# Delta-rule attention into two mixtures: warm matmuls between the opening's grams, and the next half solve on VectorE

## The chip, the cores and the metric

The kernel runs on one core of one Trainium2 chip. The metric is the device time of one execution in microseconds (us), the median of the runs.

## The reference

Three parts in a row, all in float32 at the outside; the weights come as float64.

```python
def _attn_ref(q, k, v, beta):                  # 4 batches, 8 heads, 768 positions, 48 wide
    k_n = k / (np.linalg.norm(k, axis=-1, keepdims=True) + 1e-06)
    for t in range(S):
        y[:, :, t] = einsum('bhd,bhde->bhe', q[:, :, t], state)
        v_old = einsum('bhde,bhd->bhe', state, kt)
        state = state + bt * einsum('bhd,bhe->bhde', kt, vt - v_old)

def _moe_ref(x, w_gate, w_val, w_out):         # 3072 tokens, 384 -> 1536 -> 384
    g = x @ w_gate
    return ((g * sigmoid(g)) * (x @ w_val)) @ w_out

def _moe2_ref(x, w_in, w_out):                 # 3072 tokens, 384 -> 2048 -> 384
    h = x @ w_in
    return (h * tanh(softplus(h))) @ w_out
```

## The kernel before

**The attention** goes over the 768 positions in 24 chunks of 32, three chunks to a step (t = 0 to 7). The 4 batches x 32 positions of a chunk lie on the 128 partitions. Inside a chunk the recurrence is a triangular system of 32 unknowns for each batch and head. A step needs: grams of the keys (`gram_pair`, L458; word kg), the norms of the keys (in step 0 by `square_sums`, L209 and L210, later from the gram's diagonal), and the solve. In the first two steps the solve is made in two halves of 16: `solve_half` (L276, L283) makes 15 pairs of operations, one pair for each unknown, for both halves side by side; `back_half` (L287 to L289) turns the result back with three transposes; `join` (L298) puts the halves together in two parts (words ja and jb, for the next step Ja and Jb), each of 64 small products with a ScalarE copy or a VectorE add (L309) behind.

Each chunk then runs a chain: `read` (word r: keys times state, L350, and on VectorE v minus that, L362; word y: queries times state), `att_solved` (word z: solved system times v, L370, copied into z_s once by ScalarE, L380, and once by VectorE, L376, each masked to half of the batches), `att_update` (word u: ds, L412, and the state's sum on VectorE, four operations, L429), `att_out` (word o: y from the gram of queries and keys, word qg, masked on POOL by qm, L197, and z_s; L389, ScalarE copy L398), and `x_out` (word x: three transposes, L440, ScalarE's cast xh, L445, VectorE's rest xl, L447). v is scaled by the norm on POOL (word vs, L314).

**The first mixture** takes one step of 384 tokens at a time, in groups over the 12 slices of the hidden size: gate g (L635), then ScalarE's s (L678); value v (L635), then VectorE's h (L686) and its two parts hp; and down x (L707), two slices later. Every product is three passes: high part by high, low by high, high by low. g and v have one PSUM bank each (tags "g" and "v"), so a gate waits for the s before it and a value for the h before it. The weights are converted piece by piece during the opening and the first mixture: raw data by DMA (`fetch`, L546), two ScalarE operations (`conv_begin`, L561 and L563; word cb), one VectorE operation f (`conv_step`, L572; word d), then w1h on ScalarE (L591) and w1l on POOL (L592) (`conv_tail`, word t). The next attention step's work is put between the groups. **The second mixture** (from 666 us) is all matmuls.

The order of the opening is written by hand: the string START is a list of words that `say` carries out one after the other, and each engine gets its instructions in that order. A word with ">" behind it issues the first phase of a phased step and one with ">" ahead of it the next. Besides those named: turn (transpose of the gram into g_sys, L202), scale, diag, s and S (that many pairs of the solve on VectorE, of this step and of the next), P (pairs of the next step's solve on POOL), nb, ns, ne, gam (norms in pieces), clear (POOL sets t_sys to zero), h (that many warm matmuls of zeros, L826), fetch (raw pieces by ScalarE's queue), go and done (switches). EARLY1 does the same for the first mixture: "2.3:Ja2>" is carried out 0.3 of the way into group 2.

Of the kernel before, what the change touches and what calls it, by code (L numbers as in the profile page):

```python
# [7 lines left out]
F32 = mybir.dt.float32  # L8
# [4 lines left out]
AF = mybir.ActivationFunctionType  # L13
ALU = mybir.AluOpType
# [13 lines left out]
sq0 sq1 sq2 h12 kg0 kg1 norm kg2 turn0 scale diag s1 Kg0 s2 Kg1 s2 Kg2 s2 qg0 s2 qg1 s2 qg2 s5 vs0 vs1 vs2 fetch go cb2 qm0 qm1 qm2 back0 clear  # L28
ja0> ja1> >ja0 jb0> ja2> >ja1 turn1 nb d1 >jb0 z0> >ja2 jb1> ns1 y0 >z0 u0> o0> ns2 t1 >u0 >jb1 r1> jb2> y1 ne >r1 z1> gam1 >o0 >jb2 x0> d1 >z1 u1> o1> scale diag >x0 >x0 t1 P5
>u1 r2> y2 >r2 z2> >o1 x1> d1 >z2 u2> o2> >x1 >x1 P5 t1 >u2 >o2 x2> qg3 >x2 >x2 P5 d1 t1 qm3 d1 t1 done  # L30
# [11 lines left out]
XTS = ("v", "x22", "v")  # L42
AHEAD = 1
EARLY1 = "0.7:back1 1.3:Ja0> 1.3:Ja1> 1.6:>Ja0 1.6:>Ja1 2.3:Ja2> 2.3:Jb0> 2.6:>Ja2 2.6:>Jb0 3.3:Jb1> 3.3:Jb2> 3.6:>Jb1 3.6:>Jb2 4.0:qg4 4.6:qm4 6.3:qg5 7.3:qm5"
# [15 lines left out]
def tile_delta_attention_moe_moe(  # L60
# [78 lines left out]
    z_s = at.tile([128, H, 2, D], F32, name="z_s")  # L139
# [40 lines left out]
    def k_of(n):  # L180
        return lent_k if n == 2 else k_s[n % 2]
# [183 lines left out]
    def att_solved(t, c):  # L365
# [18 lines left out]
    def att_out(t, c, hold):  # L384
        y = hold["y"]
        for h in range(H):
            for b in range(B):
# [4 lines left out]
                    rhs=z_s[bs, h, b % 2, :],  # L392
# [9 lines left out]
    def att_update(t, c):  # L402
        n = num(t, c)
        if starting:
            pss = [psm.tile([128, NP, 2, D], F32, tag=x, name="ds") for x in ("g", "x20")]
        else:
            pss = [psa.tile([128, NP, 2, D], F32, tag="a", name="ds") for _ in range(2)]
        for p in range(NP):
            for par in range(2):
                for x in range(2):  # L410
# [4 lines left out]
                        rhs=z_s[rows, 2 * p + par],  # L415
# [402 lines left out]
    fetch(0, nc.sync)  # L818
    fetch(1, nc.sync)
# [257 lines left out]
```

## Time and profile before

| | us |
|---|---|
| median of three runs | 1077.2 (1076.88 to 1077.98) |
| time of the profiled execution | 1075.51 |
| its span in the trace | 1073.4 |
| TensorE busy | 1031.5 (96%) |
| VectorE busy | 512.9 (48%) |
| ScalarE busy | 398.3 (37%) |
| POOL (GpSimd) busy | 190.2 (18%) |
| granted TensorE clock, mean over the span | 0.974 |

PE is TensorE's matmuls, DVE is VectorE, ACT is ScalarE, POOL is GpSimd, SP issues most DMAs. The granted clock is 1.00 at 2.4 GHz and 0.50 at 1.2 GHz. In a timeline row "x32" joins that many like instructions that follow each other; the time is from the first's start to the last's end, and the bracket tells how long the engine had been idle and what released it. "issue" there is a wait for nothing that the profile shows. The profile counts a small float32 product twice, as two matmuls; the lists of instructions below count it once. In the windows view a row gives the stretch, its length, and for each of PE, PEld (weight loads), DVE, ACT and POOL the busy time and the number of instructions, then the granted clock, the share of the DMA engines and GB/s; with one engine asked for, that engine alone.

### The profile page before, as it was taken

The numbers are of one execution on the slowest core, as the hardware profiler recorded it, in microseconds if no ns is written. First come the engines' busy times: TensorE is split into PE (matmuls) and PEld (weight loads), VectorE is DVE, ScalarE is ACT, GpSimd is POOL, SyncE is SP. The second block draws the span as 40 slices with busy tenths as digits, with TensorE's granted clock in tenths as the row PEclk, the third lists the DMA queues.
The fourth block names the chain that finished last, engine by engine and source line by source line (L and its number), as shares of the span: only waits on it lengthen the run. The fifth ranks groups of instructions, "written<-read, shape, count | busy, mean of one in ns | idle before, by whom it ended". The sixth has DMA issues, their size and how long they took to land.

```text
span 1073.4 us, 29430 instructions
## 1 busy us (share of the span) xinstructions
PE 1031.5 (96%) x12980; PEld 988.7 (92%) x12980; DVE 512.9 (48%) x1113; ACT 398.3 (37%) x871; POOL 190.2 (18%) x222
## 2 busy tenths in 40 slices
PE   4779799999999999999999999999999999999998
PEld 4668699889989999999999999999999999999998
DVE  8555896785884885866852243212121222212111
ACT  2259744224224234243222345333333333323232
POOL 3276632211211312212211121000000000000000
PEclk6779899999999999999999999999999999999999
DMA  7246624215206125132010044001000000100000
GB/s 213 93 152 211 202 85 154 72 45 167 72 32 188 45 72 154 44 109 68 16 60 2 16 148 140 23 7 39 24 23 23 23 31 16 38 7 30 1 23 23
DMA packets 43183, 77.52 MB, mean 72 GB/s; under 512 B 4272, under 2 KB 30000, under 8 KB 43056
## 3 DMA queue, kind: packets, MB, share of 16 engines
q1 hardware_dynamic: 41904, 72.50, 21.6%
q10 hardware_dynamic: 1152, 3.15, 0.9%
q8 instruction: 102, 1.67, 0.7%
q14 instruction: 25, 0.20, 0.1%
HBM read 59.90 MB, written 15.73 MB: 70 GB/s over the span
## 4 chain that ended last, share of the span: by engine, by line
PE 81%; DVE 6%; issue 1%; ACT 1%; ACTq 0%; DVEq 0%
PE o L635 19%; PE h L635 19%; PE v L635 12%; PE x L707 12%; PE g L635 11%; PE z L370 1%; PE ks L350 1%; PE ds L412 1%; PE y L389 1%; PE y L350 1%; DVE t_tmp L324 1%; PE gram L458 1%; DVE t_sys L331 1%; DVE h L686 1%; DVE state L429 1%
## 5 line engine op out<-in xcount | busy, mean ns | idle before, releaser
L983 DVE TENSOR_TENSOR gl<-gg,gh 128x384 fp32r<-128x384 f32 x128 | 71.4, 558 | 319.2 <-ACT gh L982 319.2
L692 POOL TENSOR_TENSOR hp<-h,hp 128x384 fp32r<-128x384 f32 x96 | 99.8, 1039 | 419.4 <-ACT hp L691 419.4
L977 ACT ACTIVATE gg<-h 128x384 f32<-128x384 f32 x128 | 62.9, 492 | 264.8 <-PE h L635 264.8
L707 PE MATMUL x<-hp,w1h 128*128 128x384 f32 x576 | 132.1, 338 | 1.4 <-ACT hp L691 1.4
L635 PE MATMUL o<-w2l,gh 128*128 128x384 f32 x384 | 129.3, 337 | 0.0
L635 PE MATMUL o<-w2h,gh 128*128 128x384 f32 x384 | 129.2, 336 | 0.0
L635 PE MATMUL o<-w2h,gl 128*128 128x384 f32 x384 | 129.2, 336 | 0.0
L691 ACT CAST hp<-h 128x384 fp32r<-128x384 f32 x96 | 49.3, 513 | 168.5 <-DVE h L686 168.4
L707 PEld LDWEIGHTS x<-hp,w1h 128*128 128x128 f32 x576 | 101.1, 188 | 3.9 <-ACT hp L691 2.1
L635 PE MATMUL h<-x2h,w2h 128*128 128x384 f32 x384 | 88.0, 337 | 0.0
L635 PE MATMUL h<-x2l,w2h 128*128 128x384 f32 x384 | 87.8, 336 | 0.0
L635 PE MATMUL h<-x2h,w2l 128*128 128x384 f32 x384 | 87.7, 336 | 0.0
L686 DVE TENSOR_TENSOR h<-s,v 128x384 f32<-128x384 f32 x96 | 52.8, 549 | 72.7 <-PE v L635 72.1
L678 ACT ACTIVATE s<-g 128x384 f32<-128x384 f32 x96 | 46.9, 489 | 101.6 <-PE g L635 101.6
L324 DVE TENSOR_TENSOR t_tmp<-t_sys,g_sys 128x31 f32<-128x31 f32 (+15 forms) x186 | 80.9, 435 | 4.5
L331 DVE TENSOR_TENSOR t_sys<-t_sys,t_tmp 128x31 f32<-128x31 f32 (+15 forms) x186 | 74.8, 402 | 6.4
L635 PE MATMUL g<-xh,w1h 128*128 128x384 f32 x288 | 69.2, 349 | 7.5 <-ACT s L678 6.5
L635 PEld LDWEIGHTS o<-w2h,gh 128*128 128x128 f32 x384 | 72.1, 188 | 0.0
L635 PEld LDWEIGHTS o<-w2h,gl 128*128 128x128 f32 x384 | 72.1, 188 | 0.0
L635 PEld LDWEIGHTS o<-w2l,gh 128*128 128x128 f32 x384 | 72.1, 188 | 0.0
L635 PE MATMUL v<-xh,w1h 128*128 128x384 f32 x288 | 67.8, 343 | 2.9 <-DVE h L686 2.6
L635 PEld LDWEIGHTS h<-x2h,w2h 128*128 128x128 f32 x384 | 68.9, 188 | 0.0
(129 smaller groups left out, 1762.9 us busy)
## 6 DMA issues: line engine op xcount, KB each, us to landing
raw<-in_w_second_dram SPq DMA_DIRECT2D x32, 384.0 KB, 4.0
raw<-in_w_first_dram SPq DMA_DIRECT2D x28, 384.0 KB, 3.9
kqT<-in_kq_dram SPq DMA_DIRECT2D x18, 512.0 KB, 3.6
w2d<-f SPq DMA_DIRECT2D x32, 192.0 KB, 4.1
w2raw<-w2d SPq DMA_DIRECT2D x16, 384.0 KB, 2.9
v<-in_v_dram SPq DMA_DIRECT2D x24, 192.0 KB, 2.9
x2d<-xs SPq DMA_DIRECT2D x24, 192.0 KB, 1.9
x2raw<-x2d SPq DMA_DIRECT2D x24, 192.0 KB, 2.4
```

The source lines that it names most:

```text
L324: nc.vector.tensor_tensor(out=tmp, in0=t_sys[:, 0:m, j:j + 1].to_broadcast([128, m, n]), in1=g_sys[:, j:j + 1, j + 1:C].to_broadcast([128, ...
L331: nc.vector.tensor_tensor(out=sl, in0=sl, in1=tmp, op=ALU.subtract)
L350: nc.tensor.matmul(out=ps[bs, 2 * p:2 * p + 2], lhsT=kqt[:, p, w, bs], rhs=state[:, b, p], start=not w or p == 0, stop=not w, skip_group_c ...
L370: nc.tensor.matmul(out=z[bs, h], lhsT=t_of(t)[bs, :, c * H + h], rhs=v_s[c][bs, h, :], start=True, stop=True)
L635: nc.tensor.matmul(out=ps, lhsT=a, rhs=b, start=start and i == 0, stop=stop and i == len(seq) - 1)
L678: nc.scalar.activation(out=s, in_=ps, func=AF.Silu)
L686: nc.vector.tensor_tensor(out=h, in0=g_t.pop(j), in1=ps, op=ALU.mult)
L691: nc.scalar.copy(out=hh, in_=h)
L692: nc.gpsimd.tensor_tensor(out=hl, in0=h, in1=hh, op=ALU.subtract)
L707: nc.tensor.matmul(out=x2[kk], lhsT=w[j][:, 6 + kk, :], rhs=m, start=j == 0 and i == 0, stop=j == J1 - 1 and i == 2,)
L977: nc.scalar.activation(out=gg, in_=ps, func=AF.Mish)
L983: nc.vector.tensor_tensor(out=gl, in0=gg, in1=gh, op=ALU.subtract)
```

## The change

1. The squares of the keys (sq) are made by ScalarE instead of VectorE.
2. 48 more warm matmuls stand between the first six and the last three grams of the opening (h18, h6, h8, h8, h5, h3), and 11 later (h2, h3, h6).
3. vs and qm (POOL) stand behind back0 and clear instead of beside the solve.
4. The next step's half solve is made by VectorE (S1, S2, S2, S2, S3 in the opening, S5 in the first mixture) instead of POOL (P5 three times); its back1 and joins come later in the first mixture.
5. jb2 moves from ahead of y1 to behind o1; o2 goes ahead of u2; the third state update (">u2"), gram qg3 and its mask qm3 move into the first mixture, and six weight pieces instead of five are converted ahead of it.
6. Raw pieces 2 and 3 are fetched by SP's queue at the start, ahead of three loads of kqT, instead of by ScalarE's queue in the opening ("fetch").
7. z_s holds its two halves one behind the other instead of interleaved by head, and the third chunk's ds and the xt use other PSUM banks.

```diff
--- before.py
+++ after.py
@@ -25,9 +25,9 @@
 FIRST = 0
 FB = 3
 START = """
-sq0 sq1 sq2 h12 kg0 kg1 norm kg2 turn0 scale diag s1 Kg0 s2 Kg1 s2 Kg2 s2 qg0 s2 qg1 s2 qg2 s5 vs0 vs1 vs2 fetch go cb2 qm0 qm1 qm2 back0 clear
-ja0> ja1> >ja0 jb0> ja2> >ja1 turn1 nb d1 >jb0 z0> >ja2 jb1> ns1 y0 >z0 u0> o0> ns2 t1 >u0 >jb1 r1> jb2> y1 ne >r1 z1> gam1 >o0 >jb2 x0> d1 >z1 u1> o1> scale diag >x0 >x0 t1 P5
->u1 r2> y2 >r2 z2> >o1 x1> d1 >z2 u2> o2> >x1 >x1 P5 t1 >u2 >o2 x2> qg3 >x2 >x2 P5 d1 t1 qm3 d1 t1 done
+sq0 sq1 sq2 h12 kg0 kg1 norm kg2 h18 turn0 scale diag s1 Kg0 h6 s2 Kg1 h8 s2 Kg2 h8 s2 qg0 h5 s2 qg1 h3 s2 qg2 s5 go cb2 back0 clear vs0 qm0 vs1 qm1 vs2 qm2
+ja0> ja1> >ja0 jb0> ja2> >ja1 turn1 nb d1 >jb0 z0> >ja2 jb1> ns1 y0 >z0 t1 u0> o0> ns1 >u0 >jb1 h2 r1> y1 ns1 ne >r1 z1> >o0 h3 gam1 scale diag d1 S1 >z1 t1 u1> o1> jb2> S2 d1
+>u1 >jb2 r2> x0> y2 S2 >x0 >r2 >x0 >o1 t1 z2> x1> S2 d1 >z2 o2> u2> >x1 >x1 t1 >o2 x2> h6 d1 >x2 >x2 t1 S3 d1 t1 done
 """
 FILL = (0.1, 0.8)
 W2AT = (4.5, 2.0, 6)
@@ -39,9 +39,9 @@
 MOST = 2
 GRAMS = ("g", "x20", "x21", "x22") * 5
 JOINS = ("x21", "x22") * 3
-XTS = ("v", "x22", "v")
+XTS = ("x22",) * 3
 AHEAD = 1
-EARLY1 = "0.7:back1 1.3:Ja0> 1.3:Ja1> 1.6:>Ja0 1.6:>Ja1 2.3:Ja2> 2.3:Jb0> 2.6:>Ja2 2.6:>Jb0 3.3:Jb1> 3.3:Jb2> 3.6:>Jb1 3.6:>Jb2 4.0:qg4 4.6:qm4 6.3:qg5 7.3:qm5"
+EARLY1 = "0.3:S5 0.9:back1 1.2:qg3 1.4:qm3 1.6:>u2 2.9:Ja0> 2.9:Ja1> 3.2:>Ja0 3.2:>Ja1 3.6:Ja2> 3.6:Jb0> 3.9:>Ja2 3.9:>Jb0 4.3:Jb1> 4.3:Jb2> 4.6:>Jb1 4.6:>Jb2 5.0:qg4 5.3:qm4 7.0:qg5 7.3:qm5"
 GRAM2 = 6.0
 
 
@@ -136,7 +136,7 @@
     ss, rs, n_sys = [t_tmp[:, C * i:C * i + C] for i in range(3)]
     state = at.tile([128, B, NP, 2, D], F32, name="state")
 
-    z_s = at.tile([128, H, 2, D], F32, name="z_s")
+    z_s = at.tile([128, 2, H, D], F32, name="z_s")
     y_s = [at.tile([128, DM], F32, name=f"y{i}") for i in range(NCH)]
 
     w2d = [dram.tile([128, 6, 128], F32, name=f"w2d{j}") for j in range(J2)]
@@ -204,9 +204,9 @@
         )
 
     def square_sums(c):
-        sq = m1.tile([128, H, D], F32, tag="h", name="sq")
-        kk = k_of(c)
-        nc.vector.tensor_tensor(out=sq, in0=kk, in1=kk, op=ALU.mult)
+        sq = m1.tile([128, 2, N], F32, tag="hp", name="sq", bufs=2)
+        sq = sq[:, 0].rearrange("p (h d) -> p h d", h=H)
+        nc.scalar.activation(out=sq, in_=k_of(c), func=AF.Square)
         nc.vector.tensor_reduce(out=n_nat[:, c * H:c * H + H], in_=sq, op=ALU.add, axis=mybir.AxisListType.X)
 
     def norms(diag):
@@ -374,10 +374,10 @@
         for x in range(2):
             if starting and x:
                 nc.vector.tensor_scalar(
-                    out=z_s[:, :, x, :], in0=z, scalar1=turn_of[:, x:x + 1], scalar2=None, op0=ALU.mult
+                    out=z_s[:, x], in0=z, scalar1=turn_of[:, x:x + 1], scalar2=None, op0=ALU.mult
                 )
             else:
-                nc.scalar.activation(out=z_s[:, :, x, :], in_=z, func=AF.Identity, scale=turn_of[:, x:x + 1])
+                nc.scalar.activation(out=z_s[:, x], in_=z, func=AF.Identity, scale=turn_of[:, x:x + 1])
         load(1, num(t + 1, c))
 
     @phased
@@ -389,7 +389,7 @@
                 nc.tensor.matmul(
                     out=y[bs, h],
                     lhsT=p_nat[num(t, c) % 5][bs, h, :],
-                    rhs=z_s[bs, h, b % 2, :],
+                    rhs=z_s[bs, b % 2, h, :],
                     start=(t == 0 and c == 0 and h == 0),
                     stop=(h % 2 == 1),
                     skip_group_check=True,
@@ -402,7 +402,8 @@
     def att_update(t, c):
         n = num(t, c)
         if starting:
-            pss = [psm.tile([128, NP, 2, D], F32, tag=x, name="ds") for x in ("g", "x20")]
+            tags = ("x20", "x21") if c == NCH - 1 else ("g", "x20")
+            pss = [psm.tile([128, NP, 2, D], F32, tag=x, name="ds") for x in tags]
         else:
             pss = [psa.tile([128, NP, 2, D], F32, tag="a", name="ds") for _ in range(2)]
         for p in range(NP):
@@ -412,7 +413,7 @@
                     nc.tensor.matmul(
                         out=pss[x][64 * par:64 * par + D, p],
                         lhsT=k_of(n)[rows, 2 * p + par, :],
-                        rhs=z_s[rows, 2 * p + par],
+                        rhs=z_s[rows, :, 2 * p + par, :],
                         start=True,
                         stop=True,
                     )
@@ -815,8 +816,8 @@
     for c in range(NCH):
         load_kq(c, slice(1, 2))
         load(1, c)
-    fetch(0, nc.sync)
-    fetch(1, nc.sync)
+    for n in range(RAWB):
+        fetch(n, nc.sync)
     for n in range(NCH, 2 * NCH):
         load_kq(n, slice(1, 2))
     heat = psm.tile([128, N], F32, tag="v", name="heat")
```

In the lists below a name with a number is one buffer: kqT_106 are the keys and queries of one chunk, lent_kq those of chunk 0, xh and xl the two parts of the mixture's input, w1h and w1l the two parts of a weight slice.

TensorE in the opening, from the first warm matmuls to join 0, before:

```order
L826 MATMUL heat<-cold 128x384 x12
L458 MATMUL gram<-lent_kq 32x32 x32
L458 MATMUL gram<-kqT_106 32x32 x32
L458 MATMUL gram<-kqT_107 32x32 x32
L458 MATMUL gram<-kqT_108 32x32 x32
L458 MATMUL gram<-kqT_109 32x32 x32
L458 MATMUL gram<-kqT_105 32x32 x32
L458 MATMUL gram<-lent_kq 32x32 x32
L458 MATMUL gram<-kqT_106 32x32 x32
L458 MATMUL gram<-kqT_107 32x32 x32
L298 MATMUL join<-lent_tn,g_nat 32x16 x64
```

and now, from the third gram on:

```order
L459 MATMUL gram<-kqT_107 32x32 x32
L827 MATMUL heat<-cold 128x384 x18
L459 MATMUL gram<-kqT_108 32x32 x32
L827 MATMUL heat<-cold 128x384 x6
L459 MATMUL gram<-kqT_109 32x32 x32
L827 MATMUL heat<-cold 128x384 x8
L459 MATMUL gram<-kqT_105 32x32 x32
L827 MATMUL heat<-cold 128x384 x8
L459 MATMUL gram<-lent_kq 32x32 x32
L827 MATMUL heat<-cold 128x384 x5
L459 MATMUL gram<-kqT_106 32x32 x32
L827 MATMUL heat<-cold 128x384 x3
```

The grams and joins keep their order; 48 matmuls of 128x384 lie between them.

VectorE from the last state update of the opening to the first h of the first mixture, before:

```order
L429 TENSOR_TENSOR state<-state,ds 48x4x2x48 x4
L447 TENSOR_TENSOR xl<-xt,xh 128x3x128
L572 SCALAR_TENSOR_TENSOR f<-raw 128x384 x3
L287 STREAM_TRANSPOSE t_nat<-t_sys 128x512
L288 STREAM_TRANSPOSE tT_nat<-t_sys 128x512
L289 STREAM_TRANSPOSE t_nat<-t_sys 128x512
L572 SCALAR_TENSOR_TENSOR f<-raw 128x384 x2
L686 TENSOR_TENSOR h<-s,v 128x384
```

and now, its last eleven rows (between xl and these stand the six operations of S3, two f, and the first three pairs of S5):

```order
L276 TENSOR_TENSOR t_tmp<-t_sys,g_sys 128x56
L283 TENSOR_TENSOR t_sys<-t_sys,t_tmp 128x2x14x2
L276 TENSOR_TENSOR t_tmp<-t_sys,g_sys 128x30
L283 TENSOR_TENSOR t_sys<-t_sys,t_tmp 128x2x15
L287 STREAM_TRANSPOSE t_nat<-t_sys 128x512
L288 STREAM_TRANSPOSE tT_nat<-t_sys 128x512
L289 STREAM_TRANSPOSE t_nat<-t_sys 128x512
L573 SCALAR_TENSOR_TENSOR f<-raw 128x384
L430 TENSOR_TENSOR state<-state,ds 48x4x2x48 x4
L573 SCALAR_TENSOR_TENSOR f<-raw 128x384
L687 TENSOR_TENSOR h<-s,v 128x384
```

The end of the solve and the third state update have come to stand ahead of the first h.

TensorE from the first v to the second v of the first mixture, before:

```order
L635 MATMUL v<-xh,w1h_82 128x384 x3
L298 MATMUL join<-t_nat,lent_g 32x16 x64
L635 MATMUL v<-xh,w1l_83 128x384 x3
L635 MATMUL v<-xl,w1h_82 128x384 x3
L635 MATMUL g<-xh,w1h_84 128x384 x3
L298 MATMUL join<-t_nat,lent_g 32x16 x32
L298 MATMUL join<-lent,tT_nat 32x16 x32
L635 MATMUL g<-xh,w1l_85 128x384 x3
L635 MATMUL g<-xl,w1h_84 128x384 x3
L635 MATMUL v<-xh,w1h_84 128x384 x3
```

and now:

```order
L636 MATMUL v<-xh,w1h_82 128x384 x3
L459 MATMUL gram<-kqT_108 32x32 x32
L636 MATMUL v<-xh,w1l_83 128x384 x3
L636 MATMUL v<-xl,w1h_82 128x384 x3
L636 MATMUL g<-xh,w1h_84 128x384 x3
L636 MATMUL g<-xh,w1l_85 128x384 x3
L636 MATMUL g<-xl,w1h_84 128x384 x3
L298 MATMUL join<-t_nat,lent_g 32x16 x64
L636 MATMUL v<-xh,w1h_84 128x384 x3
L636 MATMUL v<-xh,w1l_85 128x384 x3
L298 MATMUL join<-t_nat,lent_g 32x16 x32
L298 MATMUL join<-lent,tT_nat 32x16 x32
```

Gram qg3 lies inside the first v, and 64 of the small join products that stood ahead of the second v stand inside it.

## Rows read from the trace of the kernel before

**Rows 1.** Windows view: one stretch, each engine's busy time (count), granted clock, DMA share, GB/s.
```profile
135.00:1073.40 938.40, 930.56 (x9915) 898.84 (x9907) 425.24 (x915) 322.67 (x696) 115.78 (x112) 1.00 0.18 57
```

**Rows 2.** Waits of TensorE, 0 to 66 us: total us, times, longest us.
```profile
PE gram L458 <- issue: 10.8, 4, 3.8
PE z L370 <- issue: 2.6, 2, 2.0
PE ds L412 <- DVE z_s L376: 2.4, 3, 0.9
```

**Rows 3.** Timeline of TensorE: start us, us, line, operation, count [idle before, releaser].
```profile
13.24 1.78 PE L458 MATMUL gram<-kqT 48*32 48x32 f32 x127 [3.39 <-issue]
18.84 0.74 PE L458 MATMUL gram<-kqT 48*32 48x32 f32 x47 [3.82 <-issue]
...
22.80 1.41 PE L458 MATMUL gram<-kqT 48*32 48x32 f32 x112 [2.17 <-issue]
25.01 0.43 PE L298 MATMUL join<-lent_tn,g_nat 32*32 32x16 f32 x15 [0.81 <-DVE lent_tn L287]
26.12 1.89 PE L298 MATMUL join<-lent_tn,g_nat 32*32 32x16 f32 x113 [0.68 <-issue]
...
34.18 1.19 PE L370 MATMUL z<-v,lent_tn 32*32 32x48 f32 x49 [1.97 <-issue]
```

**Rows 4.** The page, part 3, TensorE's instruction queue: packets, MB, share.
```profile
q8 instruction: 102, 1.67, 0.7%
```

**Rows 5.** Windows view of two stretches of the opening, columns as in rows 1.
```profile
10.00:19.40 9.40, 2.34 (x178) 2.15 (x179) 8.68 (x25) 1.22 (x4) 2.66 (x3) 0.50 1.09 318
19.40:25.20 5.80, 2.82 (x217) 2.54 (x212) 5.32 (x16) 1.91 (x8) 1.85 (x3) 0.50 0.06 14
```

**Rows 6.** Timeline of TensorE: the warm matmuls, two state updates.
```profile
1.39 3.75 PE L826 MATMUL heat<-cold 128*128 128x384 f32 x12 [1.39 <-DVE floor L784]
...
36.91 1.84 PE L412 MATMUL ds<-z_s,k 64*48 64x96 f32 x32 [0.60 <-DVE z_s L376]
...
46.77 0.88 PE L412 MATMUL ds<-z_s,k 64*48 64x96 f32 x32 [0.91 <-DVE z_s L376]
```

**Rows 7.** Timeline of VectorE: two operations of the solve.
```profile
13.99 0.24 DVE L276 TENSOR_TENSOR t_tmp<-t_sys,g_sys 128x78 f32<-128x78 f32 x1
14.27 0.75 DVE L283 TENSOR_TENSOR t_sys<-t_sys,t_tmp 128x78 f32<-128x78 f32 x1
```

**Rows 8.** Timeline of TensorE: the end of the opening.
```profile
57.07 0.55 PE L440 MATMUL xt<-ident,y 128*128 128x128 f32 x3 [0.60 <-ACT y L398]
...
60.83 1.33 PE L635 MATMUL g<-xh,w1h 128*128 128x384 f32 x3 [0.96 <-ACT xh L445]
```

**Rows 9.** Timeline of ScalarE: the end of the opening.
```profile
59.96 0.43 ACT L471 COPY p<-gram 128x128 f32<-128x128 f32 x2 [2.95 <-PE gram L458]
60.28 0.50 ACT L445 CAST xh<-xt 128x384 fp32r<-128x384 f32 x1
```

**Rows 10.** Windows view, VectorE alone: middle of solve, its end, three transposes.
```profile
18.68:20.63 1.95, 1.73 (x6) 0.50 0.38 88
20.64:23.79 3.15, 2.82 (x10) 0.50 0.00 0
65.25:67.96 2.71, 2.71 (x5) 0.50 0.65 209
```

**Rows 11.** Timeline of VectorE: a state update, conversions in the first mixture.
```profile
48.60 2.06 DVE L429 TENSOR_TENSOR state<-state,ds 48x384 f32<-48x384 f32 x4
...
61.29 1.13 DVE L572 SCALAR_TENSOR_TENSOR f<-raw 128x384 uint32<-128x384 uint32 x2
64.22 1.11 DVE L572 SCALAR_TENSOR_TENSOR f<-raw 128x384 uint32<-128x384 uint32 x1 [1.80 <-POOL w1l L592]
```

**Rows 12.** Timeline of TensorE in the first mixture.
```profile
74.71 0.69 PE L635 MATMUL v<-xh,w1h 128*128 128x384 f32 x3
75.33 2.39 PE L298 MATMUL join<-lent,tT_nat 32*32 32x16 f32 x128
...
130.50 1.33 PE L635 MATMUL g<-xh,w1h 128*128 128x384 f32 x3 [5.38 <-ACT s L678]
```

## The prediction

> **What bounds the kernel now.** The view by stretches comes first. From 135 us to the end TensorE is busy for 930.56 of 938.40 us at the full clock [rows 1]; none of that code is changed, so the change can only act on the first 135 us: the opening (to the first gate group at 60.83), and the first mixture. A gain in the opening counts only if the first mixture doesn't lose it again.
>
> Next the waits of TensorE in the first 66 us: its longest are not on data but on "issue", 10.8 us ahead of grams in four waits and 2.6 us ahead of z [rows 2]. The timeline says when: at 13.24, 18.84, 22.80 and 34.18, with two more between the last two, TensorE starts again after such a wait [rows 3], and between one restart and the next there are 128 matmuls as the profile counts them (two for each small product). The instruction queue carried 1.67 MB in 102 packets, 16.4 KB each [rows 4]. I read this as instruction code arriving in blocks of 128 matmuls with their loads, and late. The periods are 5.60 us (13.24 to 18.84), 3.96 (to 22.80), and 11.38 for the three to 34.18, 3.8 each. The long one lies where the DMA engines are full (share 1.09, 318 GB/s, until 19.4; then 0.06) [rows 5]. So in the opening TensorE is bound by code, as many blocks as the program has matmuls, and VectorE's solve is a second bound close beside it: join 0 waits 0.81 us for lent_tn at 25.01 [rows 3].
>
> By its section "Instruction fetch mechanics", the page "Runtime: NRT & Kernel Launch" of the Trainium skill has the next page of 256 instructions fetched while the present one runs, the cost of a crossing mostly hidden. The trace speaks against that here (the 10.8 and 2.6 us above). Were it true of this opening, its joins would be gated by VectorE alone and rival B would hold; it stays inside B's chance.
>
> **The change part by part.** *48 warm matmuls between the grams.* Twelve took 3.75 us at the granted clock of 0.5 [rows 6], 0.31 each: 15.0 us at half clock, half of it at full. TensorE has 5.2 us of work in the 15.2 us from 10.0 to 25.2 [rows 5], so their run time nearly fits into its waits. But they are code too: join 0's first matmul is number 589 of the stream before and 637 after, that is, one block later (blocks begin at 223 and every 128 on); z0 is 845 to 908 and becomes 893 to 956. Before, z0 straddles the blocks that start at 30.02 and 34.18; now it lies in the second alone, with 35 joins ahead of it, and ends some 0.5 us later, if the blocks come as before.
>
> *Raw pieces 2 and 3 fetched at the start.* 2 x 384 KB at 318 GB/s are 2.4 us more of full DMA, just where a block is under way. SP's queue carries them ahead of three kqT loads, none of which is wanted before 40 us. The third period lies between 3.96 (no effect) and 5.60 (as the one under full DMA) [rows 3]; I take 5.4, so blocks start at 13.2, 18.8, 24.2, and then 27.5, 30.9, 34.2 at 3.3 each, the best single period being 3.32 (22.80 to 26.12). With 3.8 each z0's block would come at 35.6 (+1.4); with 22.8 and 3.3 at 32.7 (-1.5). Taken: block as before, z0 **+0.5**.
>
> *Solve undisturbed, squares on ScalarE.* vs and qm leave POOL's stretch during the solve: VectorE's 78-element operation took 0.24 us alone and 0.75 beside a POOL tensor operation [rows 7]; four such (0.69 to 0.95) make 2.1 us. With the squares gone as well lent_tn is ready near 22.6 instead of 24.9. Since join 0's block now comes at 27.5, this buys **0**; it would buy up to 2.3 if code came early. The moved vs and qm run on POOL behind back0, before r1 wants them: 0.
>
> *Contiguous z_s.* ds waits 2.4 us in three waits on VectorE's z_s, which itself stands behind ScalarE's [rows 2]. In the new order VectorE's copy still waits for ScalarE's, so the two don't run side by side: **0**, at best 0.6 for each of the three.
>
> *The end of the opening.* Before, gram qg3 stands behind the last xt on TensorE and its two copies (59.96) ahead of xh on ScalarE [rows 9]: xt ends at 57.62, the cast comes at 60.28 and g0 at 60.83 [rows 8, 9]. With qg3 in the mixture the cast follows xt at once: **-2.6**. o2 ahead of u2 takes one ds (0.81 at full clock) off the path to x2: **-0.8**. On VectorE S2 and an f stand ahead of the third z_s, and an S2 ahead of the third v; six operations of S take 1.95 us [rows 10], so four 1.3, and f 0.56 [rows 11]; against the z and copies beside them I count **+0.8** and **+0.5**. With z0's +0.5: -1.6, and g0 at **59.2** instead of 60.83.
>
> *The first mixture.* Now VectorE has the second half solve's end before it can do h0, which frees the one "v" bank for the second group's v. From g0: xl 0.56, S3 1.95 [rows 10], two f 1.13 [rows 11], S5 3.15 less 0.42 in which POOL blocked one operation, 2.73, three transposes 2.71 [rows 10], f 0.55, the third state update 2.06 [rows 11], f 0.55, h 0.55: 12.8 us. POOL's w1l runs beside it; one f took 1.11 instead of 0.56 under it [rows 11], and two or three such make 1.1 to 1.7, say 1.4. So h0 ends 14.2 after g0, at 73.4, and v1 can start. Before, v1 started at 74.71, but with 128 matmuls of joins (Ja2, Jb0) already done that are now still ahead; 128 take 2.3 (2.39 at 75.33) [rows 12]. So the mixture stands 73.4 + 2.3 - 74.7 = **+1.0 us** later. Behind that the orders are the same, with one weight piece converted sooner; the 5.38 us wait at 130.50 [rows 12] hangs on VectorE's next norms and moves along.
>
> The sum: +1.0 on the profiled execution's 1075.5 us (span 1073.4), which lies 1.7 under the median of the runs. So 1076.5 there, 1078.2 as a median. A measurement of this kernel tells about 0.2%, 2.15 us, from no change.
>
> **Rivals.** *A (forecast): opening's gain eaten by VectorE in the mixture.* As summed; with the terms at their bounds -1 to +2.1, no change that can be told.
>
> *B: faster.* Blocks come at the low bounds (z0 -1.5 - 0.5 for the block, against +0.5), and the heats hold the clock at 2.4 GHz into the first chunk: the same 32 ds took 1.84 us at 0.5 and 0.88 at 1.0 [rows 6]; ds, y and ks of chunk 0 together could give 2.2, about half of it hidden by code, 1.1. Then g0 is at about 56.6, and if POOL doesn't block (h0 13.0 after g0) v1 is at 69.6: 69.6 + 2.3 - 74.7 = -2.8, **1074.4**; lower still if part of the 5.38 us wait shrinks, to 1071.5. For it: POOL does leave the solve alone, and TensorE has the room. Against it: block periods don't shrink because TensorE is warm, and between 26 and 34 us it waits for code, during which it is idle as before.
>
> *C: slower.* VectorE's chain makes TensorE stand still before v1 (in this sum for some 3 us, since g1 ends early), and the clock falls in it. Before, after the 5.38 us wait three matmuls took 1.33 us, against 0.69 at 74.71 [rows 12]: twice. From 72.7 before ran at full clock; if it ran for another 4 to 5 us at half, that is +2.0, and a VectorE chain another microsecond later (S5 blocked by w1l as four solve operations were) +1.0: +4.0, **1081.2**. It decides if v1 starts after about 74.6. For it: VectorE is the busier engine of this stretch in the new order; against: g0 starts earlier.
>
> *D: the change doesn't do what it says.* The heats do not raise the clock of the joins, because the clock has fallen again in the waits for code; z_s stays serial. Both cost and bring nothing and are in A.
>
> **The chances.** A 0.37, B 0.34, C 0.29. B and A are close, since only the late blocks separate them; C needs one wait to last. The likeliest, A, gives 1078.2, alone from 1076.2 to 1079.3. For 8 in 10 the range goes to 1071.5 (B with its further gain) and 1082.0 (C with 0.8 more). Faster by over 0.2%: 0.34; within: 0.37; slower: 0.29.
>
> **What would show it.** In the changed profile: restarts of TensorE "issue" near 24.2, 27.5, 30.9 and 34.2, lent_tn ready near 24.9 less 2.3 and no solve operation of twice its neighbours' time; z0 ending near 36; g0 near 59.2; h0 ending near 73.4, and v1 right behind, after a wait of TensorE on VectorE's h. I am wrong to B's side if joins start before 26 or the clock row is 1.0 through ds of chunk 0, and to C's if the granted clock is 0.5 behind v1. If the stretch from 135 on differs by over 0.5 us in TensorE's busy time, the whole reading is wrong.

## The result

The change makes the kernel slower: 1085.64 us median of five runs (1083.27 to 1087.19) against 1077.2 (1075.99 to 1080.3), a ratio of 1.007 with a 95% interval of 1.0048 to 1.0092. The prediction was 1078.2, with 1071.5 to 1082.0 as its range.

| | before | after |
|---|---|---|
| profiled execution, us | 1075.51 | 1087.19 |
| its span | 1073.4 | 1085.3 |
| join 0 starts | 25.01 | 29.03 |
| z0 ends | 35.45 | 38.16 |
| last xt starts | 57.07 | 63.19 |
| first gate group (g0) starts | 60.83 | 65.33 |
| first h (h0) ends | 71.36 | 79.49 |
| second value group (v1) starts | 74.71 | 79.55 |
| third gate group (g2) starts | 81.58 | 90.36 |
| tenth gate group starts | 138.57 | 150.15 |

The spans differ by 11.9 us and the medians by 8.4: the execution profiled after lies 1.55 above its median, the one of before 1.7 below. What follows divides the 11.9 (rounded): +4.5 up to g0, +0.3 from there to v1, +3.9 from v1 to g2, +2.8 from g2 to the tenth gate group, +0.3 behind it.

The windows view of after (columns as in [rows 1]): the long rest, then the first mixture to the clock's fall, the stretch behind it, and the joins of the opening.

```profile
146.00:1085.30 939.30, 931.01 (x9927) 899.29 (x9919) 424.09 (x914) 321.64 (x692) 114.67 (x111) 1.00 0.19 57
78.40:92.00 13.60, 12.16 (x331) 10.71 (x334) 5.84 (x10) 7.81 (x18) 8.57 (x9) 0.50 0.54 161
65.30:78.40 13.10, 9.38 (x221) 8.35 (x219) 12.54 (x27) 5.77 (x14) 4.65 (x5) 0.87 0.25 76
30.60:44.20 13.60, 8.98 (x390) 7.95 (x386) 5.37 (x16) 5.43 (x13) 1.01 (x1) 0.50 0.15 47
```

The rest is as before (931.01 busy at the full clock; 930.56 in [rows 1]). In the first 13 us of the mixture VectorE is busy for 12.54 of 13.10 us, and behind it 13.6 us run at half the clock.

TensorE's waits up to 66 us, and its timeline:

```profile
PE join L298 <- issue: 4.8, 4, 1.9
PE gram L459 <- issue: 2.4, 1, 2.4
PE ds L413 <- DVE z_s L376: 1.6, 1, 1.6
```

```profile
9.49 5.23 PE L827 MATMUL heat<-cold 128*128 128x384 f32 x18
...
15.34 1.33 PE L827 MATMUL heat<-cold 128*128 128x384 f32 x6
...
19.74 0.26 PE L459 MATMUL gram<-kqT 48*32 48x32 f32 x6 [2.44 <-issue]
19.93 2.61 PE L827 MATMUL heat<-cold 128*128 128x384 f32 x8
...
23.29 1.86 PE L827 MATMUL heat<-cold 128*128 128x384 f32 x8
...
25.77 1.16 PE L827 MATMUL heat<-cold 128*128 128x384 f32 x5
...
27.55 0.79 PE L827 MATMUL heat<-cold 128*128 128x384 f32 x3
...
29.03 1.62 PE L298 MATMUL join<-lent_tn,g_nat 32*32 32x16 f32 x95
32.56 0.68 PE L298 MATMUL join<-lent_tn,g_nat 32*32 32x16 f32 x33 [1.92 <-issue]
...
36.14 0.71 PE L298 MATMUL join<-lent_tn,g_nat 32*32 32x16 f32 x33 [1.52 <-issue]
36.65 1.51 PE L370 MATMUL z<-v,lent_tn 32*32 32x48 f32 x64
...
63.19 0.90 PE L441 MATMUL xt<-ident,y 128*128 128x128 f32 x3
63.74 1.74 PE L827 MATMUL heat<-cold 128*128 128x384 f32 x6
65.33 0.68 PE L636 MATMUL g<-xh,w1h 128*128 128x384 f32 x3
...
72.10 1.33 PE L636 MATMUL g<-xh,w1h 128*128 128x384 f32 x3 [2.58 <-ACT s L679]
...
79.55 1.33 PE L636 MATMUL v<-xh,w1h 128*128 128x384 f32 x3 [2.29 <-DVE h L687]
...
141.20 1.33 PE L636 MATMUL g<-xh,w1h 128*128 128x384 f32 x3 [5.41 <-ACT s L679]
```

The grams' waits for code (the waits for "issue", read as the prediction reads them) have shrunk from 10.8 us to 2.4 [rows 2]. TensorE is at work on the warm matmuls meanwhile: from 9.49 to 30.6 it has one wait. Its joins begin 4.0 us later than in [rows 3], and z0 ends 2.7 us later. v1 waits for h as the prediction said, but at 79.55. The wait of 5.4 us is there again, 10.7 us later than in [rows 12].

VectorE and ScalarE of after, two places: the third chunk, and the mixture up to h0.

```profile
57.23 0.98 DVE L276 TENSOR_TENSOR t_tmp<-t_sys,g_sys 128x126 f32<-128x126 f32 x1
...
58.45 0.55 DVE L573 SCALAR_TENSOR_TENSOR f<-raw 128x384 uint32<-128x384 uint32 x1
60.08 0.62 DVE L376 TENSOR_SCALAR z_s<-z,turn_of 128x384 f32<-128x384 f32 x1 [1.07 <-ACT z_s L380]
...
65.12 1.15 DVE L276 TENSOR_TENSOR t_tmp<-t_sys,g_sys 128x128 f32<-128x128 f32 x1
...
69.64 0.94 DVE L283 TENSOR_TENSOR t_sys<-t_sys,t_tmp 128x96 f32<-128x96 f32 x1
...
73.29 1.09 DVE L287 STREAM_TRANSPOSE t_nat<-t_sys 128x512 f32<-128x512 f32 x1
...
76.27 2.05 DVE L430 TENSOR_TENSOR state<-state,ds 48x384 f32<-48x384 f32 x4
...
78.94 0.56 DVE L687 TENSOR_TENSOR h<-s,v 128x384 f32<-128x384 f32 x1
```

```profile
59.08 0.34 ACTq L547 DMA_DIRECT2D raw<-in_w_first_dram  x1
59.46 0.58 ACT L380 ACTIVATE z_s<-z,turn_of 128x384 f32<-128x384 f32 x1 [1.58 <-PE xt L441]
```

z2 is done at 58.33, but ScalarE's z_s comes at 59.46, behind a DMA issue that by the times follows the f (58.45 to 59.00), which stands on VectorE behind S2 with one operation blocked to 0.98. And between g0 and h0 VectorE hardly rests.

### The profile page after: what moved, and what is told of

Its sections match the earlier page's. It is cut to its first block, busy times and chain, and to the rows that moved or that the text cites. A ratio compares the mean times of both kernels' runs of the same rounds, so it can differ in the third digit from the quotient of the medians.

```text
span 1085.3 us, 29539 instructions
## 1 busy us (share of the span) xinstructions
PE 1050.3 (97%) x13039; PEld 1004.5 (93%) x13039; DVE 518.5 (48%) x1140; ACT 400.6 (37%) x874; POOL 177.4 (16%) x192
## 3 DMA queue, kind: packets, MB, share of 16 engines
q1 hardware_dynamic: 42192, 73.29, 21.9%
## 4 chain that ended last, share of the span: by engine, by line
PE 80%; DVE 6%; issue 1%; ACT 1%; ACTq 0%; DVEq 0%
PE o L636 19%; PE h L636 19%; PE v L636 12%; PE x L708 11%; PE g L636 11%; PE z L370 1%; PE ks L350 1%; PE ds L413 1%; PE y L389 1%; PE y L350 1%; DVE t_tmp L324 1%; PE gram L459 1%; DVE t_sys L331 1%; DVE h L687 1%; DVE state L430 1%
```

## The experiments

Fifteen runs, with the kernel before run beside them each time (its median 1076.7 to 1077.3):

| run | median, us | ratio to before (95%) | g0 | transposes | h0 ends | v1 | g2 |
|---|---|---|---|---|---|---|---|
| before | 1077.2 | | 60.83 | 65.25 | 71.36 | 74.71 | 81.58 |
| after | 1085.6 | 1.0070 (1.0048 to 1.0092) | 65.33 | 73.29 | 79.49 | 79.55 | 90.36 |
| e1_no_heats | 1087.0 | 1.0094 (1.0080 to 1.0108) | 62.97 | 70.46 | 76.70 | 76.76 | 87.88 |
| e2_pool_solve | 1086.4 | 1.0093 (1.0079 to 1.0107) | 64.79 | 73.67 | 79.88 | 79.93 | 90.76 |
| e3_before_heats | 1079.5 | 1.0024 (1.0010 to 1.0037) | 66.60 | 71.00 | 76.71 | 80.07 | 87.02 |
| e4_neither | 1082.7 | 1.0053 (1.0040 to 1.0066) | 58.24 | 67.83 | 74.05 | 74.11 | 85.35 |
| e5_behind_h0 | 1090.5 | 1.0126 (1.0113 to 1.0139) | 65.22 | 80.23 | 74.40 | 74.45 | 83.45 |
| e6_behind_h0_no_heats | 1089.4 | 1.0112 (1.0098 to 1.0125) | 63.00 | 78.03 | 72.20 | 72.25 | 81.27 |
| e7_warm_in_waits | 1089.8 | 1.0110 (1.0094 to 1.0125) | 66.68 | 74.17 | 80.41 | 86.24 | 94.26 |
| e8_before_tiny_code | 1077.6 | 1.0007 (0.9992 to 1.0022) | 62.51 | 67.00 | 73.10 | 77.41 | 84.05 |
| e9_grouped_pool | 1077.0 | 1.0002 (0.9991 to 1.0013) | 60.84 | 63.44 | 70.79 | 74.22 | 81.05 |
| e10_grouped_vector | 1081.1 | 1.0037 (1.0024 to 1.0050) | 67.22 | 68.90 | 77.46 | 81.77 | 88.67 |
| e11_end_of_opening | 1075.1 | 0.9990 (0.9979 to 1.0000) | 56.77 | 62.58 | 69.00 | 71.92 | 80.73 |
| e12_warm_own_bank | 1084.8 | 1.0075 (1.0061 to 1.0089) | 63.85 | 72.18 | 78.44 | 80.50 | 88.94 |
| e13_earlier_solve | 1074.0 | 0.9977 (0.9968 to 0.9985) | 56.38 | 60.71 | 68.27 | 71.64 | 79.70 |
| e14_late_joins | 1078.4 | 1.0017 (1.0008 to 1.0027) | 59.55 | 63.41 | 69.64 | 70.41 | 81.05 |
| e16_small_parts | 1075.6 | 0.9995 (0.9986 to 1.0004) | 58.90 | 62.74 | 70.52 | 73.91 | 80.77 |

The stage times are those of each run's profile, which is one execution. Four kernels share the opening of after (after, e5, e7, e12), and their g0 lies between 63.85 and 66.68, so a difference of less than some 3 us between two single stage times is not firm.

"Transposes" is when VectorE starts the three transposes of the next step's solve (L287), that is, when the half solve is done and VectorE has come to them. Of the columns it orders the medians best, from e13 (60.71, the fastest) to e5 (80.23, the slowest); e3 lies some 4 us below a straight line through them and e1 some 4 us above it. The runs changed other things as well, so this alone proves no cause; the pairs below do more.

### The warm matmuls (e1, e3, e8)

```diff
-sq0 sq1 sq2 h12 kg0 kg1 norm kg2 h18 turn0 scale diag s1 Kg0 h6 s2 Kg1 h8 s2 Kg2 h8 s2 qg0 h5 s2 qg1 h3 s2 qg2 s5 ...
+sq0 sq1 sq2 h12 kg0 kg1 norm kg2 turn0 scale diag s1 Kg0 s2 Kg1 s2 Kg2 s2 qg0 s2 qg1 s2 qg2 s5 ...
```

> The changed kernel without the 48 warm matmuls of the opening grams (the 11 later ones stay). Theory H (the warm matmuls delay the opening: they run ahead of the grams and make one more block of code): z0 ends near 35.5 us instead of 38.2, g0 comes some 2.7 us earlier (near 62.6), h0 14.2 us after it, and the end 2.7 us earlier: about 1083. Theory S (the late VectorE chain of the half solve is what costs): the same time as the changed kernel within 1 us, 1085 to 1086, because what the opening gains is waited for later. Theory C (they hold the clock and so gain): slower than the changed kernel by 1 to 3 us.

> The kernel before with the 48 warm matmuls alone added at the same places. Theory H: z0 ends 2 to 3 us later and the time is 1079 to 1080. Theory C (the clock pays for them): grams and joins at 2.4 GHz, z0 not later than before, 1075 to 1077. Theory S says nothing of it: 1077 to 1078.

e3 is that line's other direction on the kernel before; in e8 each of the 48 has 8 columns instead of 384.

> The kernel before with 48 matmuls of 8 columns where the changed kernel has the 48 warm ones of 384: as much code, nearly no time of their own. If the warm matmuls cost by their code (join 0 moves into the next block of 128): z0 ends 1 to 2.5 us later than the 35.5 of before, 1078 to 1080. If they cost by their run time ahead of the grams: z0 within 0.5 us, 1076.5 to 1077.5.

Alone on the kernel before, they cost 2.6 us by the ratio (0.24%): join 0 starts at 28.98, z0 ends at 38.41, almost the times of after. So in the opening theory H holds. The execution profiled of e3 lies 2.3 us above its median, and ahead of its g0 stand three waits for code (0.69, 0.76 and 2.19 us) where before has two (0.59 and 1.38), so its later stage times say less.

But without the warm matmuls the changed kernel was not faster (1087.0; its interval overlaps that of after). g0 came 2.4 us and v1 2.8 us earlier, and all of it was gone by the seventh gate group, at 121.49 against 121.54: a wait for code opened behind the fourth gate group, and 3.4 us there ran at half clock. The timeline of e1 there, and the same wait in e4, where the clock is at 1.00:

```profile
100.07 1.18 PE L370 MATMUL z<-v,t_nat 32*32 32x48 f32 x55 [1.07 <-issue]
101.18 1.33 PE L636 MATMUL g<-xh,w1l 128*128 128x384 f32 x3
```

```profile
96.74 1.01 PE L370 MATMUL z<-v,t_nat 32*32 32x48 f32 x55 [1.01 <-issue]
```

From the fourth gate group to the v behind it after takes 4.51 us, e4 5.22 and e1 6.63: some 0.7 us of the loss go with the wait, 1.4 with the half clock.

e8 does not tell code from run time. Its premise was wrong: 18 matmuls of 8 columns took 4.00 us, 0.22 each, not nearly nothing, and all 48 took 11.2 us against 13.1 in e3.

```profile
10.44 4.00 PE L892 MATMUL heat<-cold 128*128 128x8 f32 x18
```

Its z0 ended at 35.75, 0.3 us after before's, and its time can't be told from before's. Most of its lead on e3 is that its one long wait for code in the grams ended at 18.09, against 19.72.

### Where the half solve is made (e2, e4)

```diff
-... d1 S1 >z1 t1 u1> o1> jb2> S2 d1 >u1 >jb2 r2> x0> y2 S2 >x0 ... x1> S2 d1 ... t1 S3 d1 t1 done
+... d1 P1 >z1 t1 u1> o1> jb2> P2 d1 >u1 >jb2 r2> x0> y2 P2 >x0 ... x1> P2 d1 ... t1 P3 d1 t1 done
-EARLY1 = "0.3:S5 0.9:back1 ...
+EARLY1 = "0.3:P5 0.9:back1 ...
```

> The changed kernel with the next step's half solve on POOL again, at the same places of the order (S1, S2, S2, S2, S3, S5 become P). Theory S: VectorE has 13 us of work less between z1 and h0, the third z_s no longer stands behind it, h0 comes 8 to 10 us after g0 instead of 14.2, and the end 4 to 7 us earlier, 1079 to 1082; only the 2.5 us of the warm matmuls stay. Theory H: at most 1.5 us earlier, 1084 to 1086, because POOL's solve then ends as late and the joins wait for it.

> The changed kernel without the 48 warm matmuls and with the half solve on POOL: squares on ScalarE, vs and qm behind the solve, early raw pieces, gram qg3 and the third state update in the mixture stay. If H and S are both right and add up: 1076 to 1079, about the kernel before or a little below. If one of the two hides behind the other, the same as the better of the two alone, 1079 to 1083. If neither is the cause: above 1083.

The diff is e2's; e4 leaves out the 48 warm matmuls as well. e2 is no faster than after, so theory S falls as I put it. In small pieces between POOL's w1l operations the solve takes from 48.04 to 73.63, where that of before took from 48.31 to 62.87, and VectorE's transposes wait for it: they start at 73.67, as late as after (73.29). VectorE in e2, then TensorE in e4:

```profile
73.67 1.05 DVE L287 STREAM_TRANSPOSE t_nat<-t_sys 128x512 f32<-128x512 f32 x1 [7.35 <-POOL t_sys L283]
```

```profile
63.56 0.79 PE L636 MATMUL g<-xh,w1h 128*128 128x384 f32 x3 [1.14 <-ACT s L679]
...
69.02 2.11 PE L298 MATMUL join<-t_nat,lent_g 32*32 32x16 f32 x128 [3.63 <-DVE t_nat L287]
74.11 1.33 PE L636 MATMUL v<-xh,w1h 128*128 128x384 f32 x3 [2.97 <-DVE h L687]
```

e4 is the telling one: its g0 comes at 58.24, 2.6 us ahead of before, and its g2 3.8 us behind. Opening gained, mixture lost, and the clock is at half from 68.6 to 85.7. Its 1082.7 is 4.3 us below e1 and 3.7 below e2, clear of their intervals; against after it is 2.9 by the medians and 1.8 by the ratios, whose intervals overlap.

### Order and clock in the first mixture (e5, e6, e7, e12)

```diff
-EARLY1 = "0.3:S5 0.9:back1 1.2:qg3 1.4:qm3 1.6:>u2 2.9:Ja0> 2.9:Ja1> ...
+EARLY1 = "1.2:qg3 1.4:qm3 1.6:>u2 2.05:S5 2.1:back1 4.9:Ja0> 4.9:Ja1> ...
```

> The changed kernel with the last five pairs of the half solve and its three transposes behind the first h of the mixture instead of ahead of it, the joins two groups later, and grams qg4 and qg5 behind the joins. Theory V (the work on VectorE ahead of h0 is what makes v1 late, and TensorE's wait there loses the clock): h0 ends about 8.7 us after g0 instead of 14.2, v1 starts near 75 instead of 79.6, no half clock behind it, 1077 to 1081. Theory O (the late opening, g0 at 65.3 instead of 60.8, is what counts): at most 1.5 us better than the changed kernel, 1084 to 1086, because h1 and the joins then wait for the same VectorE work.

> The same with the 48 warm matmuls of the grams left out as well. Theory V with the warm matmuls as a second cost (z0 2.7 us earlier): g0 near 62.5, v1 near 72, 1075 to 1078. Rival (without the warm matmuls the clock falls in the mixture and eats the gain, as their removal alone brought nothing): 1079 to 1083.

h0 and v1 came where theory V said (74.40 and 74.45 in e5, 72.20 and 72.25 in e6), and the time got worse by 5 us; both medians lie above every range that I gave. The wait moved to the joins, and from there to the read of the next step. TensorE in e5:

```profile
81.42 2.10 PE L298 MATMUL join<-t_nat,lent_g 32*32 32x16 f32 x128 [2.42 <-DVE t_nat L287]
...
88.33 1.51 PE L350 MATMUL ks<-state,kqT 128*32 128x96 f32 x32 [2.83 <-ACT lent L311]
```

Its fourth gate group starts at 104.3, against 99.9 after and 89.7 before. So h0's place alone is not the cause. What is left is when the half solve is done (the transposes start at 80.23 here), since the joins need it as much as h0 needs VectorE; e14 below tests that.

e7 and e12 put 12 and 12 (10) warm matmuls ahead of g1 and v1, e7 into a shared PSUM bank, e12 into one nobody held.

> The changed kernel with 12 more warm matmuls ahead of g1 and 12 ahead of v1, where TensorE waits 2.6 and 2.3 us. Theory C (of the 10.7 us that the changed kernel is behind at 141 us some 3.5 are the 13.7 us at half clock that begin at 78.4): v1 stays at 79 to 80, the clock stays at 1.00 behind it, g2 comes near 87 instead of 90.4, and the time is 1081 to 1083. Rival (the half clock there hides under VectorE's and ScalarE's work): g2 is as late, 1085 to 1087.

> The changed kernel with 12 warm matmuls ahead of g1 and 10 ahead of v1 again, now into a PSUM bank that nobody holds there, so that they run inside TensorE's waits and not behind them. Theory C (the half clock from 78.4 to 92.0 costs about 3 us): v1 at 79.5 to 80.2, the clock 1.00 from 76 on, g2 near 87.5 to 88, 1082 to 1083.5. Rival: no change, 1085 to 1086.

In e7 they waited for the bank and ran behind the waits (3.69 and 3.42 us on the path):

```profile
73.11 3.69 PE L832 MATMUL heat<-xh 128*128 128x384 f32 x12 [2.11 <-ACT p L472]
...
83.02 3.42 PE L832 MATMUL heat<-xh 128*128 128x384 f32 x12 [2.39 <-ACT lent L311]
```

v1 to g2 then took 8.02 us instead of 10.81, so the half clock there is worth about 2.8 us, but the 6.7 us that v1 lost were more, and the time lies above both ranges. In e12 they ran inside the waits, yet a wait for code (1.51 at 77.02) came ahead of the second lot and the clock was at half from 76.2 to 83.0 all the same; v1 to g2 took 8.44, and at 1084.8 it can't be told from after. A cheap way to hold the clock there was not found.

### When the half solve is done (e9, e10, e14)

e9 is e4 with POOL's solve in three blocks of five pairs and the mixture's events as in the kernel before; e10 has those blocks on VectorE; e14 is e9 with the changed kernel's late joins.

```diff
-... d1 P1 >z1 ... jb2> P2 d1 ... y2 P2 >x0 ... x1> P2 d1 ... t1 P3 d1 t1 done
+... d1 P5 >z1 ... jb2> P5 d1 ... y2 P5 >x0 ... x1> d1 ... t1 d1 t1 done
-EARLY1 = "0.3:P5 0.9:back1 1.2:qg3 1.4:qm3 1.6:>u2 2.9:Ja0> ...
+EARLY1 = "0.7:back1 1.2:qg3 1.3:Ja0> 1.3:Ja1> 1.4:qm3 1.6:>Ja0 1.6:>Ja1 1.6:>u2 ...
```

> The changed kernel without the 48 warm matmuls, with the half solve on POOL in three blocks of five pairs that start as early as g_sys and t_sys allow, and with the transposes and joins in the mixture where the kernel before has them (transposes 0.7, joins 1.3 to 3.6). Kept are squares on ScalarE, vs and qm behind the solve, early raw pieces, qg3 and the third state update in the mixture. Theory V (what stands on VectorE ahead of h0, and when the half solve is done, decides): g0 near 58.3 as without both, the solve done near 60, h0 near 69 to 70, v1 near 72, 1073.5 to 1076. Rival (the third state update ahead of h0 and the clock take it back): 1077 to 1081.

> The same with the three blocks of the half solve on VectorE. If VectorE's solve costs only where it stands ahead of h0: the solve is done before g0, g0 1 to 2 us later than in the run beside it (59.5 to 60.5), v1 within 1 us of that run's, 1074 to 1077. If it costs in the chain of the three chunks as well: g0 at 62 or later, 1078 to 1082.

> The run with the half solve in grouped blocks on POOL, with transposes and joins in the mixture where the changed kernel has them (transposes 0.9, joins 2.9 to 4.6) instead of where the kernel before has them. If the solve's end is what decided between the split and the grouped POOL solve (1082.7 and 1077.0): 1076.5 to 1078.5. If the place of the joins did: 1081 to 1083, with v1 waiting as long and the half clock behind it.

Grouping ends POOL's solve at 59.85 instead of 67.80 (e4) and brings 5.7 us: e9 stands level with the kernel before. Theory V had 1073.5 to 1076 for it; its g0 came at 60.84 instead of 58.3. e14 divides the 5.7. With the grouped solve and late joins it is 4.3 us ahead of e4, and the transposes start 4.4 us sooner (63.41 for 67.83); the joins' place is worth the other 1.4, which is not clear of the intervals (1.0008 to 1.0027 and 0.9991 to 1.0013). VectorE in e14:

```profile
63.41 1.09 DVE L287 STREAM_TRANSPOSE t_nat<-t_sys 128x512 f32<-128x512 f32 x1
```

The same blocks on VectorE cost 4.1 us more than on POOL (e10 against e9), and they do it in the opening: g0 at 67.22 instead of 60.84 (more than the medians differ by, since e10's profiled execution lies 1.9 us above its median and e9's 1.8 below). Grouping helps on VectorE as well: e10, with the early joins, is 5.9 us below e1, which has the same engine and no warm matmuls of the grams either.

### The parts that gain (e11, e13, e16)

e11 is the kernel before with only the end of the opening changed; e13 has POOL's solve released earlier too; e16 is e13 with the small parts of the change. The diff is e13's against before (qg3, qm3 and >u2 also come into the mixture at 1.2, 1.4 and 1.6, and the third ds into the banks that the change gives it); e11 leaves scale, diag and the three P5 where they were.

```diff
-... >r1 z1> gam1 >o0 >jb2 x0> d1 >z1 u1> o1> scale diag >x0 >x0 t1 P5 >u1 r2> y2 >r2 z2> >o1 x1> d1 >z2 u2> o2> >x1 >x1 P5 t1 >u2 >o2 x2> qg3 >x2 >x2 P5 d1 t1 qm3 d1 t1 done
+... >r1 z1> gam1 scale diag P5 >o0 >jb2 x0> d1 >z1 u1> o1> >x0 >x0 t1 P5 >u1 r2> y2 >r2 z2> >o1 x1> d1 >z2 o2> u2> >x1 >x1 P5 t1 >o2 x2> >x2 >x2 d1 t1 d1 t1 done
```

> The kernel before with the end of the opening alone changed: o2 ahead of u2, gram qg3, its mask and the third state update moved into the first mixture at the changed kernel's places (1.2, 1.4, 1.6). My terms -2.6 and -0.8: g0 near 57.5 instead of 60.8. Theory V: POOL's half solve still ends near 63 and the transposes near 68, then f and the state update come ahead of h0, so h0 is no earlier than the 71.4 of before: 1076.5 to 1079. Rival (an earlier g0 carries through): 1073.5 to 1075.5.

> The kernel before with the end of the opening as in the run that changed it alone, and POOL's half solve released as soon as the next step's norms are there (scale and diag right behind gam1, the three blocks of five pairs one w1l earlier each). Theory V: the solve ends near 60 instead of 62.6, the transposes near 63, the join's wait of 4.0 us on t_nat in the first v shrinks to 1 to 2, h0 near 66.5 to 67.5, 1072 to 1074. Rival (scale and diag ahead of the second z_s push the chain back as much, or the clock takes it): 1075 to 1076.5.

> The run with the earlier half solve on POOL, in the changed kernel's code: squares on ScalarE, vs and qm behind the solve, raw pieces 2 and 3 fetched at the start, z_s in contiguous halves. My prediction counted these at 0 each (join 0 waits for code, not for VectorE): within 1 us of the run beside it. If they are worth something: 1 to 3 us less; if the early raw fetch delays the code blocks: 1 to 2 us more.

e11's median is 2.2 us lower than that of the kernel beside it, 1.1 by the ratio, and its interval just reaches 1 (0.9979 to 1.0000): g0 comes 4.1 us earlier, and the first join then waits 4.0 us on the transposes. Theory V had h0 no earlier than 71.4; it ended at 69.00, and the time lies in the rival's range. TensorE in e11:

```profile
63.80 2.12 PE L298 MATMUL join<-t_nat,lent_g 32*32 32x16 f32 x128 [3.99 <-DVE t_nat L287]
```

e13 beats both kernels: 1073.99 us, 0.23% below before (0.9968 to 0.9985), inside what was expected. Not all went as expected: POOL's solve ends at 58.45, but the join still waits 3.85. An f of VectorE that waits for POOL's w1l stands ahead of the transposes, and when the first of these is done (61.76) the join is not free yet: the profile puts its wait down to ScalarE's copy of gram qg3 (p), which came into the mixture: gram and join take their PSUM banks from the same two there (tag "a"). VectorE, ScalarE and TensorE in e13:

```profile
59.45 1.33 DVE L572 SCALAR_TENSOR_TENSOR f<-raw 128x384 uint32<-128x384 uint32 x1 [1.46 <-POOL w1l L592]
60.71 1.05 DVE L287 STREAM_TRANSPOSE t_nat<-t_sys 128x512 f32<-128x512 f32 x1
...
62.96 0.42 ACT L471 COPY p<-gram 128x128 f32<-128x128 f32 x2
...
63.27 2.12 PE L298 MATMUL join<-t_nat,lent_g 32*32 32x16 f32 x128 [3.85 <-ACT p L471]
```

e16 is 1.6 us above e13, outside the 1 us that I gave it: squares, vs and qm, the early raw pieces and z_s bring nothing together, and cost a little here; which of them does wasn't tried.

## Why the prediction was wrong

**The step that failed first: the warm matmuls' run time.** I wrote that "their run time nearly fits into its waits", with 15.0 us of them at half clock, half of that at full, and 5.2 of other work set against 15.2 us of time. At half clock those numbers say 20.2 in 15.2. The half was wrong too: at a granted clock of 1.00 five took 1.16 us (25.77), 0.23 each and not 0.16 ([rows 6], where my 0.31 comes from, show no clock), so that 48 are 11 us even then, with 10.0 of waits for them; and I counted 0. Measured, the six groups take 13.0 us together, TensorE has one wait of 2.44 us from 9.49 to 30.6, and join 0 starts 4.0 us late. Of that, 3.1 lie behind the wait (9.3 us from its end to join 0, 6.4 of them warm matmuls, against 6.2 from 18.84 before); the other 0.9 is the wait's end, which falls anywhere from 17.5 to 20.3 in the runs without the 48. e3 shows the same by itself.

I had looked for the cost in the code block that they add, +0.5. That reading of the blocks was sound (restarts at 32.56, 36.14 and 39.71, 3.6 us apart, with 128 and 127 matmuls between them), but the blocks could only start from where the grams ended. z0 +2.7 instead of +0.5. What the early raw pieces add to it stays open: without the 48, z0 ends at 35.15 to 36.97 in the seven runs that have the small parts of the change, at 34.12 to 35.46 in the three that have not (before, e11, e13).

**The half solve in the chunks: mis-sized.** I counted +0.8 and +0.5 for S2 ahead of the third z_s and v. From z0's end to the last xt it is 23.9 us in e1 with the solve on VectorE and 21.7 in e4 with it on POOL: 2.3, for the same order. Other executions of the same openings put it between 1 and 3 us (25.0 in e6 with the solve on VectorE; with the warm matmuls 24.4 to 25.7 in after, e5, e7 and e12, against 23.8 in e2). The rest of the +3.4 is not divided further. Part is a queue that I did not follow: ScalarE's z_s at 59.46 stands behind the conversion's DMA, which came after VectorE's f.

**The end of the opening: -2.6 came as -1.6** (xt to g0 is 2.14 instead of 3.76 us), since six warm matmuls of the change (h6, 1.74 us at 63.74) stand ahead of g0, 0.7 us longer than xh needs, and the xt took 0.90 us instead of 0.55. I left out those 11 altogether. Without them both terms came: in e11 xt to g0 is 1.11 (-2.65), and from z2's end to the xt it is 3.02 instead of 3.69 (-0.67 for my -0.8). With z0 +2.7, the chunks +3.4 and this -1.6, g0 is 4.5 late where I had -1.6: 65.33 for 59.2.

**VectorE's chain to h0: right in sum.** I said 14.2 us from g0; it is 14.16, and v1 follows 0.06 us later. Two terms are off and nearly cancel: xl starts 0.7 us ahead of g0, and POOL's w1l blocks the two S pieces (S3 from 65.12 to 67.87, S5 from 68.73 to 73.25) for some 2.6 us instead of 1.4. That they cancel is luck.

**Behind v1: rival C came in, on top.** Its point was v1 later than 74.6, and v1 was at 79.55. The half clock from 78.4 to 92.0 with the joins still to do makes v1 to g2 3.9 us longer, where I had 2.3 for the joins alone; g2 to the tenth gate group, which I had as unchanged, is 2.8 us longer, of which 1.4 lie in the first of these groups, whose start is still at half clock, and 0.9 in the one behind the wait at 141.20. Against C's own price of 2.0 e7 shows 2.8. C's time of 1081.2 was too low because the opening that it stands on was 6.1 us later than I had it. (Rival B's "-1.5 - 0.5 for the block" has a wrong sign; its 56.6 goes by -1.5 + 0.5.)

**Right:** the rest from 135 us on is unchanged; VectorE's solve runs undisturbed (its 78-element operations take 0.24 each, against 0.75 in [rows 7]), ends 1.9 us earlier, and buys nothing for join 0. Its lent_tn was ready at 22.99 and join 0 came 6 us later. z_s stays serial: VectorE waited 5.7 us in three waits for ScalarE's. The squares gained nothing there: VectorE's sums waited for them, and the solve started 0.2 us later. The waits for code in the joins (4.8 us in four) speak once more against the rule of the Trainium skill ("Runtime: NRT & Kernel Launch", Instruction fetch mechanics) that such a crossing is mostly hidden. And D's first half: the joins from 30.6 on and z0 ran at half clock (0.50 from 30.6 to 44.2), in spite of the matmuls ahead of them.

**The cause, then.** Shown: the half solve taken from POOL's contiguous blocks, so that it ends late (its transposes start at 73.29 after, 65.25 before, [rows 10]) and, on VectorE, also stands in the way of the chunks. From e1 the way back to the time of before has two steps, each clear of the intervals: blocks together and joins early, still on VectorE, 5.9 us (e10), and then POOL instead of VectorE, 4.1 (e9, level with before). For the blocks without the joins' place there is the pair on POOL, e4 and e14: 4.3 us. Shown too: the warm matmuls, 2.6 us where the mixture can follow (e3), 3.7 from e2 to e4. Warm matmuls and VectorE's solve don't add up: taking out either alone brings nothing (e1, e2), both together 2 to 3 us (e4). What after would take with its blocks together and its warm matmuls left in was not measured.

## What to carry to other kernels

Filler work has a price even on an engine that waits for most of its time: add its run time to the work of the stretch and compare with the stretch, before asking what else it does. A solve that another engine made off to the side cost nothing that shows as long as it ended in time (e9); cut into pieces between that engine's other waits it took much longer (25.6 us in e2 against 14.6 before), so look at when its last piece ends and who waits for that. And an earlier start of the next stage is worth only what the next bound leaves: in e11 g0 came 4.1 us earlier for 1 to 2 us at the end.

## What the runs showed of the hardware

A matmul of 8 columns with its 128x128 weight load took 0.22 us (e8), three quarters of one of 384 columns in the same place (5.23 us for 18 after, 0.29 each). Waits of TensorE for code come in the mixture as well, among its small matmuls (1.07 us in e1, 1.51 in e12), and their place differs with the instructions ahead of them: after has 0.29 us inside a gram at 103.81, e1, without the 48, 1.07 inside z at 100.07. With the warm matmuls in the opening the granted clock was at 1.00 from 13.5 to 20.3 and from 23.8 to 30.6, where before had 0.50 up to 25.2 [rows 5]; it was at 0.50 again for the 13.6 us of joins, z and ds behind them, in which TensorE was busy for 8.98 us. Their length went with it: the eight at 19.93, nearly all at 0.50, took 2.61 us, and the eight at 23.29, from 23.8 on at 1.00, 1.86.
